# Row stores issued one at a time behind three points of a group, a pool of its own for the scores' two PSUM banks, and another order of slot 0's half blocks

## The chip, the cores and the metric

The kernel runs on one core of a Trainium2 chip. The metric is the device time of one execution in microseconds. The program schedules TensorE (PE), VectorE (DVE), ScalarE (ACT) and GpSimd (POOL) by hand: on each of these engines instructions run in the order in which the program writes them. SyncE (SP) only issues loads.

## The reference

Chunked softmax attention feeds a mixture of eight experts in which each row goes to one expert:

```python
# q, k, v: 8 x 8 heads x 576 x 64, chunks of 64
scores = scale * np.matmul(q_c, k_c.transpose(0, 1, 2, 4, 3))
attn = np.exp(scores - np.max(scores, axis=-1, keepdims=True))
attn = attn / (np.sum(attn, axis=-1, keepdims=True) + 1e-09)
x = np.matmul(attn, v_c)            # laid out as 4608 rows of 512
...
logits = x @ w_gate                 # 512 -> 8
expert_idx = np.argmax(logits, axis=1)
# gate_w: softmax of the logits at expert_idx
for e in range(E):
    xe = x[expert_idx == e]
    h = np.maximum(xe @ w1[e], 0.0) # 512 -> 1024
    out[expert_idx == e] = gate_w[...] * (h @ w2[e])
```

## The kernel before

**Attention.** The 4608 rows are 36 tiles of 128. A pass g of the loop `for g in range(NG)` (18 passes, here called groups) works on two tiles and holds three stages at once: the scores of g (64 small matmuls, L229, into the two banks of `pair["S"]`), then for group g-1 the transposes of its exponentials (`attn_t`, L272), the row sums (`soft_c`), and the weighted product (`attn_v`, 64 small matmuls, L281, into `pair["X"]`), and for group g-2 the transposes of its finished rows (`x_t`, L304) and the router's logits (`logits`, L316, copied to `lp`, L903). "The product of group 10" is the one that is issued in pass 10. The program also splits the first expert's weights into a high and a low part there: `cast(g)` lets ScalarE copy half a chunk (L81) and GpSimd subtract (L82), and issues the next load.

**Routing and row stores.** Tiles are routed in batches of 4, 8, 8, 4, 4, 4, 4. `route` is a generator whose steps (`"c"`, `"v"`, `"a"`, `"t"`) the program places by `advance` and `small_op`; after its last vector steps each tile of the batch stands in the list `waiting` with the row numbers `di`. `store(n, after)` takes n of them: GpSimd copies one column of `after` (L418), so that it waits for that tile, and then issues one indirect transfer a tile (L421) that scatters 128 rows of 528 floats to the DRAM tile `xd`, sorted by expert. A group has two such points, behind the row sums and behind the copy of the logits; each issues one store, or two when more than four tiles are waiting:

```python
store(2 if len(waiting) > 4 else 1, su[:, 0, :])
...
store(2 if len(waiting) > 4 else 1, st_l[gl][:, 0:1])
```

**The tail and slot 0.** The experts' rows are worked in slots of 256 rows. `early(0)` finds slot 0's rows when the first three batches are stored and gathers them (`gather(0)`, L541); `make_xt(0)` transposes them (L564) and splits them (`xhi` L566 on ScalarE, `xlo` L567 on VectorE, then `ids`, L555 and L556). `slot_0` is a generator: 16 steps in the order `BLOCKS`, a "1" step a block of the first gemm (12 matmuls, L584), a "2" step one of the second (6 matmuls, L660 to L662), each in two halves. `filler(n)` issues n halves between the steps of the last groups' attention and routing; `halves` counts those left. The last route, the stores of the last batch, the tables of slots (`tables`, L749 to L841), the gather of slot 1's extra rows (`gather_x(1)`) and the loads of the next expert's weights (`load_w`, L526) follow, and the remaining halves run beside them.

**Banks.** The eight PSUM banks are one pool `psa`: S and X of two banks, T, Q, L and K of one. Slot 0's first gemm alternates between a bank of S and T, its second gemm adds up in the two banks of X. Behind slot 0 the pool is closed and all eight banks are taken again under new names for the later slots, which run to the end: slot 1 begins with the transposes of its extra rows (`make_xt_x`, L573, bank T), their split (L575, L576) and the first gemm (`gemm1_x`, L591). `finish` (L666) scales a slot's result and scatters it to the output.

## Time and profile before

| | us |
|---|---|
| median of 3 runs | 650.45 (649.5 to 650.96) |
| the profiled execution | 648.89 |
| its span, first to last instruction | 647.1 |
| TensorE busy in the span | 591.4 |
| VectorE, ScalarE, GpSimd busy | 420.9, 286.5, 275.2 |
| mean granted clock of TensorE | 0.968 of full speed |

The attention groups take the first 135 us of the span, the tail with slot 0 the stretch to about 180 us, the later slots the rest. Times in the rows are microseconds from the start of the span; merged instructions of one line stand in one row with their count. "issue" as a releaser is time in which the engine waited for nothing that the profile shows, and a wait for several semaphores is put down to the one that came last by the profile.

### The profile page before, as it was taken

How to read it: one execution, taken by the hardware profiler on the slowest of the kernel's cores; microseconds unless marked ns; L12 is line 12 of the kernel's file. 1: busy time of each engine (PE TensorE's matmuls, PEld its weight loads, DVE VectorE, ACT ScalarE, POOL GpSimd, SP SyncE). 2: the span in 40 equal slices, each digit the busy share in tenths (PEclk: the TensorE clock that was granted, in tenths of full speed). 3: DMA queues.
4: the chain of work that ended last, by engine and by line, in shares of the span. 5: the costliest groups of instructions: out<-in, count | busy, mean ns of one | idle time of the engine just before them, and what ended most of it. 6: DMA issues, size and time to landing. Idle time of an engine off the chain costs nothing.

```text
span 647.1 us, 14596 instructions
## 1 busy us (share of the span) xinstructions
PE 591.4 (91%) x5775; PEld 518.6 (80%) x5775; DVE 420.9 (65%) x831; ACT 286.5 (44%) x523; POOL 275.2 (43%) x287
## 2 busy tenths in 40 slices
PE   7697898987979999999999999998999999999980
PEld 5575676766879989988798878997889999989970
DVE  6696868774556667765476566776547667767760
ACT  2465746552123445444354344553435545445530
POOL 2024345565514437434174143743407346437431
PEclk9899979789989999999999999999999999999995
DMA  8989789533465332146036211356602055111100
GB/s 324 375 282 364 256 294 297 194 118 122 159 226 169 135 116 81 55 147 213 6 111 222 82 38 44 106 209 229 206 2 91 18 181 183 58 49 35 34 5 30
DMA packets 31901, 94.87 MB, mean 147 GB/s; under 512 B 11488, under 2 KB 11488, under 8 KB 28192
## 3 DMA queue, kind: packets, MB, share of 16 engines
q0 software_dynamic: 20880, 60.74, 27.6%
q1 hardware_dynamic: 10896, 32.53, 14.3%
q8 instruction: 71, 1.16, 0.7%
q14 instruction: 54, 0.44, 0.2%
HBM read 122.65 MB, written 19.96 MB: 220 GB/s over the span
## 4 chain that ended last, share of the span: by engine, by line
PE 73%; issue 9%; DMA 8%; ACT 3%; DVE 2%; another core or an unknown queue 1%; POOL 1%; SPq 0%; POOLq 0%; DVEq 0%; ACTq 0%
PE psS L584 14%; PE psS L591 8%; DMA out_y<-y,oid 7%; PE psX L584 4%; PE psX L281 4%; PE psL L661 4%; PE psR L660 4%; PE psL L660 4%; PE psR L661 4%; PE psR L662 4%; PE psL L662 4%; PE psS L229 3%; PE psX L591 2%; PE psT L304 2%; PE psQ L304 1%
## 5 line engine op out<-in xcount | busy, mean ns | idle before, releaser
L75 DVE TENSOR_TENSOR wlo<-raw,whi 128x1024 fp32r<-128x1024 f32 x134 | 163.8, 1223 | 38.4 <-ACT whi L74 33.2
L526 POOL DMA_INDIRECT raw<-in_w,widx x71 | 73.7, 1038 | 195.9 <-DVE wlo L75 156.1
L74 ACT CAST whi<-raw 128x1024 fp32r<-128x1024 f32 x134 | 140.2, 1046 | 0.1
L604 ACT ACTIVATE hh<-psS 128x256 fp32r<-128x256 f32 x106 | 40.7, 384 | 171.7 <-PE psS L584 87.9
L584 PE MATMUL psS<-xlo,whi 128*128 128x256 f32 x328 | 92.9, 283 | 1.8 <-DVE xlo L567 1.8
L584 PE MATMUL psS<-xhi,whi 128*128 128x256 f32 x328 | 92.9, 283 | 0.5 <-DVE xlo L567 0.5
L584 PE MATMUL psS<-xhi,wlo 128*128 128x256 f32 x328 | 92.8, 283 | 0.0
L541 POOL DMA_INDIRECT xg<-xd,idx x58 | 81.5, 1405 | 22.9 <-issue 14.6
L609 DVE SCALAR_TENSOR_TENSOR hl<-psS,hh 128x256 fp32r<-128x256 f32 x106 | 44.8, 422 | 65.6 <-ACT hh L604 36.0
L667 POOL DMA_INDIRECT out_y<-y,oid x40 | 53.6, 1340 | 45.2 <-DVE y L666 39.7
L584 PEld LDWEIGHTS psS<-xlo,whi 128*128 128x128 f32 x328 | 62.6, 191 | 4.5 <-DVE xlo L567 2.0
L584 PEld LDWEIGHTS psS<-xhi,whi 128*128 128x128 f32 x328 | 62.6, 191 | 4.2 <-ACT xhi L566 0.7
L584 PEld LDWEIGHTS psS<-xhi,wlo 128*128 128x128 f32 x328 | 62.6, 191 | 0.0
L660 PE MATMUL psL<-whi,hh 128*128 128x512 f32 x136 | 55.0, 405 | 0.0
L661 PE MATMUL psL<-wlo,hh 128*128 128x512 f32 x136 | 53.8, 396 | 0.0
L660 PE MATMUL psR<-whi,hh 128*128 128x512 f32 x136 | 53.5, 393 | 0.0
L661 PE MATMUL psR<-wlo,hh 128*128 128x512 f32 x136 | 53.3, 392 | 0.0
L662 PE MATMUL psR<-whi,hl 128*128 128x512 f32 x136 | 53.1, 391 | 0.0
L662 PE MATMUL psL<-whi,hl 128*128 128x512 f32 x136 | 53.1, 391 | 0.0
L82 POOL TENSOR_TENSOR wlo<-raw,whi 128x512 fp32r<-128x512 f32 x16 | 20.4, 1276 | 61.4 <-ACT whi L81 61.4
L421 POOL DMA_INDIRECT xd<-xb,di x32 | 31.8, 994 | 15.1 <-issue 7.7
L281 PE MATMUL psX<-vb,at 64*64 64x64 f32 x1152 | 29.3, 235 | 8.1 <-issue 7.7
(237 smaller groups left out, 1218.1 us busy)
## 6 DMA issues: line engine op xcount, KB each, us to landing
vb<-in_v SPq DMA_DIRECT2D x18, 512.0 KB
kb<-in_k SPq DMA_DIRECT2D x17, 512.0 KB
qt<-in_q SPq DMA_DIRECT2D x17, 512.0 KB
raw<-in_w SPq DMA_DIRECT2D x16, 256.0 KB
raw<-in_w,widx POOLq DMA_INDIRECT x71
xg<-xd,idx POOLq DMA_INDIRECT x58
out_y<-y,oid POOLq DMA_INDIRECT x40
kb<-in_k SPq DMA_DIRECT2D x2, 256.0 KB
```

Source lines behind the costliest of these rows:

```text
L74: nc.scalar.copy(hi, src)
L75: nc.vector.tensor_tensor(lo, src, hi.bitcast(F32), ALU.subtract)
L281: nc.tensor.matmul(px[po, m, fo], at[pi, i, hp, po], vb[g % NB][pi, i, fi], start=True, stop=True, tile_position=at_)
L526: nc.gpsimd.indirect_dma_start(out=raw[c][:, :], out_offset=None, in_=w, in_offset=bass.IndirectOffsetOnAxis(ap=widx[:, u, c:c + 1], axis= ...
L541: nc.gpsimd.indirect_dma_start(out=t[:, :], out_offset=None, in_=xd[0:rows, :], in_offset=bass.IndirectOffsetOnAxis(ap=place(u, h), axis=0 ...
L584: nc.tensor.matmul(ph, a, b[:, kc, 0:BLK], start=kc + i == 0, stop=kc + i == 5)
L591: nc.tensor.matmul(ph, a[par][kc][:, f * 128:(f + 1) * 128], b[:, kc, 0:BLK + n], start=kc + i == 0, stop=kc + i == 5)
L609: nc.vector.scalar_tensor_tensor(hl, ph, 0.0, hh.bitcast(F32), ALU.max, ALU.subtract)
L660: nc.tensor.matmul(py, hh, wh, start=f == 0, stop=False)
L661: nc.tensor.matmul(py, hh, wl, start=False, stop=False)
L662: nc.tensor.matmul(py, hl, wh, start=False, stop=f == 7)
L667: nc.gpsimd.indirect_dma_start(out=outs[m], out_offset=bass.IndirectOffsetOnAxis(ap=oid[u % 3][0:n, m:m + 1], axis=0), in_=y, in_offset=No ...
```

## The change

Three things change together.

The stores: every point issues one store, however many tiles are waiting, and there is a third point in a group, behind the exponential of the group's own scores, used when more than two tiles are waiting. In the tail stores of two and of all waiting tiles become stores behind single tiles (the transposed exponentials, the row sums, the transposed rows, the logits), mostly one each; the last batch's are issued one for every two halves of slot 0, each behind a small copy on ScalarE (`tick`). `gather_x(1)` moves behind the first two weight loads. The weight halves are split one group earlier (`j = g - 1`), so that the last group splits none.

The banks: S has its own pool, closed behind the last maximum of the scores; its two banks then rotate for slot 0's first gemm and for the later slots. The other six banks stay as they are to the end: U and V (formerly the pair X) take the second gemm's sums in all slots, the later slots' third bank of the first gemm is L.

The half blocks: slot 0's first gemm uses the two S banks alone, and the halves between the steps of the tail are 1, 2, 1, 1, 1, 1, 2, 1, 1 in place of 1, 1, 2, 1, 1, 1, 1, so that 11 instead of 8 are issued before the loop that ends the tail. The last transposes of rows (`x_t`) stand behind one more of them.

```diff
--- before.py
+++ after.py
@@ -83,21 +83,24 @@
 
 
 
-    pa = ExitStack()
-    psa = pa.enter_context(tc.tile_pool(name="psa", bufs=1, space=PSUM))
-    pair = {x: psa.tile([P, 2, 512], F32, name=f"ps{x}") for x in "SX"}
+    psa = ctx.enter_context(tc.tile_pool(name="psa", bufs=1, space=PSUM))
+    pair = {"X": psa.tile([P, 2, 512], F32, name="psX")}
     one = {x: psa.tile([P, 512], F32, name=f"ps{x}") for x in "TQLK"}
-    slots = {"S": [pair["S"][:, 0, :], pair["S"][:, 1, :]], "X": [pair["X"][:, 0, :]],
-             "Y": [pair["X"][:, 1, :]], "TQ": [one["T"], one["Q"]], **{x: [one[x]] for x in "TQLK"}}
+    c2 = ExitStack()
+    pss = c2.enter_context(tc.tile_pool(name="pss", bufs=1, space=PSUM))
+    pair["S"] = pss.tile([P, 2, 512], F32, name="psS")
+
+    slots = {"U": [pair["X"][:, 0, :]], "V": [pair["X"][:, 1, :]], "X": [one["L"]],
+             "TQ": [one["T"], one["Q"]], **{x: [one[x]] for x in "TQLK"}}
     turns = {x: 0 for x in slots}
     psum = []
 
-    def bank(tag, shape, bufs=1):
+    def bank(tag, shape):
         n = 1
         for x in shape[1:]:
             n *= x
-        if psum:
-            t = psum[0].tile([P, 512], F32, name=f"ps{tag}", tag=tag, bufs=bufs)
+        if tag == "S":
+            t = psum[0].tile([P, 512], F32, name="psS", tag="S", bufs=2)
         else:
             t = slots[tag][turns[tag] % len(slots[tag])]
             turns[tag] += 1
@@ -130,7 +133,7 @@
     ones = const.tile([P, P], BF16, name="ones")
     nc.vector.memset(ones, 1.0)
 
-    pw = bank("X", [P, P])
+    pw = bank("U", [P, P])
     for _ in range(WARM):
         nc.tensor.matmul(pw, ones, ones, start=True, stop=True)
     iota_i = xg[0][0][:, 0:P].bitcast(I32)
@@ -190,6 +193,7 @@
     nc.gpsimd.memset(oh_b, 0.0)
 
     behind = kv.tile([P, 1], F32, name="behind")
+    moments = kv.tile([P, 16], F32, name="moments")
     cb = kv.tile([P, NBAT, E], F32, name="cb")
     ce = kv.tile([P, E, NBAT], F32, name="ce")
 
...
@@ -629,14 +633,14 @@
             f = BLOCKS[:i].count(step)
             flush()
             if step == "1":
-                ph = bank("ST"[f % 2], [P, BLK])
+                ph = bank("S", [P, BLK])
                 gemm1_pe(0, f, ph, range(2))
                 yield
                 gemm1_pe(0, f, ph, range(2, 4))
                 lo_.append((ph, relu_hi(ph)))
             else:
                 if py is None:
-                    py = [bank(x, [P, D]) for x in "XY"]
+                    py = [bank(x, [P, D]) for x in "UV"]
                 gemm2(0, f, h0[f], 0, py)
                 yield
                 gemm2(0, f, h0[f], 1, py)
@@ -917,7 +921,7 @@
 
     def cast(g):
 
-        j = g - 2
+        j = g - 1
         if 0 <= j < 16:
             split_half(j // 2, j % 2, j // 4 % 2)
         j = g + 1
@@ -937,13 +941,19 @@
         if ga >= 0:
             at = attn_t(st_e[ga])
             su = soft_c(st_e.pop(ga))
-            store(2 if len(waiting) > 4 else 1, su[:, 0, :])
+            store(1, su[:, 0, :])
         if gl >= 0:
             st_x[gl] = x_t(gl, xb[gl * G // RB % XB])
         st_e[g] = soft_a(ps)
         if g + 1 < NG:
             soft_b(st_e[g])
+            if len(waiting) > 2:
+                store(1, st_e[g][:, 0, 0, 0:1])
             cast(g)
+        else:
+
+            c2.close()
+            psum.append(ctx.enter_context(tc.tile_pool(name="psum", bufs=1, space=PSUM)))
         advance("t")
         pauses()
         if g + 1 < NG:
@@ -953,10 +963,9 @@
         logits(gl)
         if g + 1 == NG:
             soft_b(st_e[g])
-            cast(g)
         if ga >= 0:
             if gl >= 0:
-                store(2 if len(waiting) > 4 else 1, st_l[gl][:, 0:1])
+                store(1, st_l[gl][:, 0:1])
             ri = soft_d(su)
             x_out(ga, px, ri, xb[ga * G // RB % XB])
         small_op(2)
@@ -970,50 +979,63 @@
     g = NG - 1
     sel_(g - 2)
     advance("c")
-    make_xt(0, banks="SX")
+    make_xt(0, banks="SS")
     small_op(5)
     ex = st_e.pop(g)
     at = attn_t(ex)
-    store(2)
+    store(1, at[:, 0, 0, 0:1])
     filler(1)
     su = soft_c(ex)
+    store(1, su[:, 0, :])
     advance("a")
     st_x[g - 1] = x_t(g - 1, xb[(g - 1) * G // RB % XB])
+    store(1, st_x[g - 1][:, 0, 0:1])
     pauses()
     small_op(7)
     advance("a")
     px = attn_v(g, at)
-    filler(1)
+    filler(2)
     ri = soft_d(su)
     x_out(g, px, ri, xb[g * G // RB % XB])
+    logits(g - 1)
+    store(1, st_l[g - 1][:, 0:1])
+    filler(1)
     advance("t")
-    logits(g - 1)
     small_op(5)
     advance("a")
-    store(NMAX)
-    filler(2)
-    flush()
+    filler(1)
     st_x[g] = x_t(g, xb[g * G // RB % XB])
+    store(2, st_x[g][:, 0, 0:1])
     sel_(g - 1)
+    filler(1)
     side_op(4)
     logits(g)
-    side_op(4)
-    pauses()
+    store(2, st_l[g][:, 0:1])
+    assert stored.issuperset(range(TE[1]))
     filler(1)
     sel_(g)
     advance("c")
-    filler(1)
+    side_op(4)
+    pauses()
+    filler(2)
     pauses()
     small_op(7)
     advance("a")
     filler(1)
-    side_op(5)
     advance("t")
     filler(1)
     small_op(5)
     advance("a")
-    store(NMAX)
-    assert len(stored) == NTILE
+    side_op(5)
+    ticks = [0]
+
+    def tick():
+
+        t = moments[:, ticks[0]:ticks[0] + 1]
+        nc.scalar.copy(t, pid[:, 0:1])
+        ticks[0] += 1
+        return t
+
     while active:
         for x in "cat":
             advance(x)
@@ -1022,7 +1044,10 @@
         side_op(3)
         if halves[0] > 5:
             filler(1)
-    gather_x(1)
+        if halves[0] % 2:
+            store(1, tick())
+    store(NMAX)
+    assert len(stored) == NTILE
     load_w(2, 0)
     load_w(2, 1)
 
@@ -1035,20 +1060,17 @@
     yp = ctx.enter_context(tc.tile_pool(name="yp", bufs=1))
     hx = ctx.enter_context(tc.tile_pool(name="hx", bufs=HB))
     hq = ctx.enter_context(tc.tile_pool(name="hq", bufs=1))
+    filler(2)
+    gather_x(1)
+    filler(2)
     for c in range(2, 4):
         load_w(2, c)
     filler(halves[0] - 4)
-    make_xt(1, banks="QT")
+    make_xt(1, banks="QK")
     filler(5)
-    pa.close()
-    psum.append(ctx.enter_context(tc.tile_pool(name="psum", bufs=1, space=PSUM)))
-
-    for tag, n in (("S", 2), ("L", 1), ("R", 1), ("Q", 1), ("K", 1), ("T", 1), ("X", 1)):
-        bank(tag, [P, 512], n)
-
     def slot(u, kd, nxt):
         par = wset(u)
-        py = [bank("LR"[m], [P, D]) for m in range(2)]
+        py = [bank("UV"[m], [P, D]) for m in range(2)]
         if u > 1:
             gather(u + 2)
```

## Rows read from the trace of the kernel before

**Rows 1.** The page's second part: TensorE's busy time and its granted clock in tenths, in 40 slices of the span.

```profile
PE   7697898987979999999999999998999999999980
...
PEclk9899979789989999999999999999999999999995
```

**Rows 2.** The table of windows, all engines: the stretch in us from the span's start, its length, then for PE, PEld, DVE, ACT and POOL the busy us and the number of instructions, the granted clock of TensorE, the busy share of the transfer engines, and GB/s.

```profile
78.50:92.00 13.50, 11.45 (x225) 9.10 (x228) 6.50 (x9) 6.22 (x12) 6.68 (x9) 0.75 0.91 318
...
92.00:109.00 17.00, 15.74 (x415) 12.70 (x407) 16.02 (x32) 11.08 (x27) 8.14 (x13) 1.00 0.86 272
...
109.00:122.00 13.00, 11.23 (x233) 9.36 (x235) 9.07 (x26) 6.58 (x13) 6.47 (x10) 0.74 0.66 227
...
187.00:280.00 93.00, 93.00 (x565) 84.67 (x565) 63.20 (x126) 42.24 (x72) 42.84 (x34) 1.00 0.32 103
```

**Rows 3.** The timeline of TensorE through the attention groups: start, duration of the merged instructions, line, operands, count, and in brackets the idle time before and what ended it.

```profile
27.96 0.49 PE L272 MATMUL psT<-ident,ex 128*128 128x128 f32 x3 [2.88 <-issue]
...
72.27 1.16 PE L281 MATMUL psX<-vb,at 64*64 64x64 f32 x64
...
73.36 0.64 PE L316 MATMUL psL<-xT,wg_sb 128*32 128x256 f32 x8
...
78.51 0.93 PE L281 MATMUL psX<-vb,at 64*64 64x64 f32 x41
...
83.10 0.64 PE L316 MATMUL psL<-xT,wg_sb 128*32 128x256 f32 x8
...
83.67 1.98 PE L229 MATMUL psS<-kb,qt 64*64 64x64 f32 x64
...
92.33 1.20 PE L229 MATMUL psS<-kb,qt 64*64 64x64 f32 x64
...
98.00 0.50 PE L281 MATMUL psX<-vb,at 64*64 64x64 f32 x15 [0.38 <-issue]
...
99.00 1.16 PE L229 MATMUL psS<-kb,qt 64*64 64x64 f32 x64
...
109.05 0.80 PE L281 MATMUL psX<-vb,at 64*64 64x64 f32 x38
...
113.36 0.64 PE L316 MATMUL psL<-xT,wg_sb 128*32 128x256 f32 x8
...
126.41 0.80 PE L281 MATMUL psX<-vb,at 64*64 64x64 f32 x37
...
128.77 0.64 PE L316 MATMUL psL<-xT,wg_sb 128*32 128x256 f32 x8
```

**Rows 4.** The timeline of GpSimd: three of the stores of attention rows (the first and the fourth of group 9 and 10, and one of group 12).

```profile
77.09 1.00 POOL L421 DMA_INDIRECT xd<-xb,di  x1
...
81.02 0.99 POOL L421 DMA_INDIRECT xd<-xb,di  x1 [0.30 <-issue]
...
96.70 0.99 POOL L421 DMA_INDIRECT xd<-xb,di  x1 [0.55 <-issue]
```

**Rows 5.** The timelines of GpSimd, VectorE and TensorE around the first gather and the transposes of slot 0's rows.

```profile
126.75 0.99 POOL L421 DMA_INDIRECT xd<-xb,di  x1 [0.16 <-issue]
...
130.70 1.04 POOL L541 DMA_INDIRECT xg<-xd,idx  x1 [0.73 <-PE psS L229]
...
138.91 1.30 POOL L82 TENSOR_TENSOR wlo<-raw,whi 128x512 fp32r<-128x512 f32 x1
...
138.60 1.64 DVE L556 SCALAR_TENSOR_TENSOR oid<-msk,xg 128x1 int32<-128x1 f32 x1
...
136.82 0.60 PE L564 MATMUL psX<-ident,xg 128*128 128x128 f32 x4
...
140.90 0.39 PE L584 MATMUL psS<-xlo,whi 128*128 128x256 f32 x1 [1.77 <-DVE xlo L567]
```

**Rows 6.** First the chain of work that ended last, where slot 0's half blocks run without a wait (start, us, what); then the timelines of TensorE and ScalarE at the last route.

```profile
163.92 1.44 PE psS L584 x12
...
166.75 1.43 PE psT L584 x12
...
153.08 0.51 PE L894 MATMUL psL<-sel_g,lp 128*128 128x8 f32 x4
...
158.07 0.18 PE L376 MATMUL psK<-oh_b,tri 128*128 128x40 bf16 x1 [2.96 <-DVE oh_b L357]
...
156.71 0.18 ACT L340 COPY lg<-psL 128x32 f32<-128x32 f32 x1 [3.81 <-remote]
```

**Rows 7.** The timelines of GpSimd (the last stores, gather_x) and TensorE (slot 0's last matmul and slot 1's first), then one row of the table of windows.

```profile
163.73 1.05 POOL L421 DMA_INDIRECT xd<-xb,di  x1 [2.57 <-DVE tot L766]
...
167.67 0.97 POOL L421 DMA_INDIRECT xd<-xb,di  x1 [0.30 <-issue]
...
171.26 1.05 POOL L541 DMA_INDIRECT xg<-xd,idx  x1 [2.62 <-DVE kind L841]
...
178.46 0.39 PE L662 MATMUL psX<-whi,hl 128*128 128x512 f32 x1
...
181.41 0.63 PE L573 MATMUL psT<-ident,xg 128*128 128x128 f32 x4 [2.56 <-DVE y L666]
...
182.75 1.65 PE L591 MATMUL psS<-xhi,whi 128*128 128x384 f32 x4 [0.72 <-ACT xhi L575]
...
178.00:180.00 2.00, 0.85 (x4) 0.38 (x2) 0.98 (x4) 0.59 (x1) 0.00 (x0) 1.00 0.98 401
```

More of the change, by code (lines that the diff above doesn't have):

```diff
@@ L561, in make_xt @@
         for h in range(2) if part is None else (part,):
-            pg = bank(banks[h], [P, 4, 128], 2 if banks == "SS" else 1)
+            pg = bank(banks[h], [P, 4, 128])
             for kc in range(4):
@@ L586, in gemm1_x @@
     def gemm1_x(par, f, n, hh=None, hl=None):
-        ph = bank("X", [P, BLK + n]) if f % 3 == 2 else bank("S", [P, BLK + n], 2)
+        ph = bank("X", [P, BLK + n]) if f % 3 == 2 else bank("S", [P, BLK + n])
         for i, (a, b) in enumerate(((w_hi, xhi), (w_lo, xhi), (w_hi, xlo))):
@@ L612, in gemm1 @@
     def gemm1(par, f, hh=None, hl=None):
-        ph = bank("X", [P, BLK]) if f % 3 == 2 else bank("S", [P, BLK], 2)
+        ph = bank("X", [P, BLK]) if f % 3 == 2 else bank("S", [P, BLK])
         gemm1_pe(par, f, ph)
```

## The prediction

> **What bounds the kernel now.** I read the page first: TensorE is busy in nearly every slice, but not in the first third, where the granted clock also dips [rows 1]. The table of windows says how to split that third: between the disturbed stretches the clock stands at 1.00, in 78.5 to 92 and 109 to 122 us it averages 0.75 and 0.74, and from 187 us on TensorE is busy all the time at full clock [rows 2]. So a microsecond saved before 187 us is a microsecond at the end, and nothing can be saved behind it. Then I took TensorE's timeline through the attention groups. A group's weighted product (64 small matmuls, L281) takes 1.09 us from its start to the next matmul where nothing disturbs it; in group 10 it breaks into pieces, "issue" before each, and needs 78.51 to 83.10, which is 4.59 us; in group 14 it needs 109.05 to 113.36, 4.31 us; in group 16 2.36 us; in group 12 one gap of 0.38 us [rows 3]. GpSimd's timeline beside it shows what these have in common: four stores without a pause around the product of group 10, one store beside that of group 12 [rows 4]; the product at 72.27, with no store near, is whole. Behind the two long breaks the granted clock is at the lower of its two levels, 1.2 GHz: the scores at 83.67 take 1.98 us where those at 99.00 take 1.16, and from the scores at 83.67 to the next at 92.33 it is 8.66 us, from there to 99.00, with one gap taken off, 6.29 us. Last, the tail: TensorE waits 1.77 us for xlo, 2.96 us for route's one-hot, 2.56 and 0.72 us at the start of slot 1 [rows 5 to 7].
>
> **The change, part by part.** The profiled execution took 648.89 us (span 647.1); the median of the runs is 650.45, so 1.56 is added at the end.
>
> *Stores, one at a time.* Their number, bytes and issue time stay (36 of about 1 us each on GpSimd). Followed by hand, the eight stores of a large batch leave at eight points of groups 9 to 12 (13 to 16), one each, and the last leaves at the same point of the same group as before; no point has two. What is there to gain is 3.50 us (group 10), 3.22 (group 14), 1.27 (group 16), 0.38 (group 12), and the lower clock, 2.4 in group 11 and, estimated from the equal clock of the two windows [rows 2] and a little lower because routing's matmuls share that group, 2.0 in group 15: 12.8 us in all. What takes its place: the store behind the row sums still falls on the weighted product in groups 10, 11, 12, 14, 15 and 16. One alone costs 0.38, which I put on group 12; in the other five the store of the logits' point before it is adjacent, and I take two gaps, 0.8: 5 x 0.8 + 0.4 = 4.4. The new point, behind the exponential, lies just ahead of the next group's scores, which are 64 matmuls of the same kind: five such stores at 0.38 are 1.9. That leaves 6.3, a gain of 6.5 us. Bounds: all 17 stores at the price of group 10 (3.50 / 4 = 0.88) and the clock down twice (4.4) make 19.4, a loss of 6.6; six single gaps and nothing at the scores make 2.3, a gain of 10.5. I take the middle because the nearest row, group 12, has single stores in just this place. The extra one-column copies (at most 0.2 us each) and the split that now stands behind them delay only GpSimd: who waits for the split's result is slot 0, tens of microseconds later.
>
> *Weight halves split one group earlier.* The same 16 splits; the loads run groups ahead, except the first, which has nine loads of 0.5 MB ahead of it on SP (4.7 MB, some 12 us at the 400 GB/s of [rows 7]) and lands about when group 1 wants it: 0 to 1 us of ScalarE's time, which then still waits for transposes. I take 0. What goes is the split in group 17: there the oid step of VectorE took 1.64 us until GpSimd's split at 138.91 was over, and TensorE waited 1.77 for the xlo behind it [rows 5].
>
> *Slot 0's rows.* gather(0) waits until every store ahead of it has landed: the store at 126.75 ended at 127.74, the gather began at 130.70, 2.96 later [rows 5]. In the new order group 16 has one more store, behind its exponential, ahead of the gather. I place its end near 129.5, so the gather begins near 132.4, 1.7 later; its second half, 1.35 behind, ends its issue near 134.7 and would land some 3 us later, near 137.7, where TensorE wants it at 136.8 [rows 5]. Against that stand 0.5 on ScalarE and 1.5 on VectorE from the missing split. Net about 1 us of the 1.77 is saved, and, as an estimate, 1 us of lower clock behind it; but the last weighted product now runs at full clock beside a queue of stores, and I charge 1.0. Net 1 us, bounds -2 and +4.
>
> *Half blocks laid anew.* Ten halves instead of seven stand ahead of the last route's matmuls. A half costs 0.71 us (two steps from 163.92 to 166.75 [rows 6]), so they cover 2.1 of the 2.96 wait; two buffers for the half blocks instead of a bank shared with x_t remove a wait of x_t for hl. ScalarE's copy of the logits came 3.1 us late although TensorE had finished ("remote", [rows 6]); it may come late again. 2.1 of cover, the idle 2.96 and some slow clock behind it are 6 to 7; I take 5 us, bounds 2 and 8. With the 1 us above, slot 0's last matmul would end at 178.9 - 6 = 172.9 [rows 7].
>
> *Banks that stay.* L573 waited for y only because all banks changed hands at once; bank T is now free, so 2.56 us would go. But gather_x is now behind two weight loads on GpSimd's queue. Followed through [rows 7]: the last batch's stores had to wait for gather(1) and began at 163.73. gather(1) needs the stores behind the last logits, which I place 2.4 us earlier (half of the 5, as the logits stand in the middle of the stretch), so the four stores run 161.3 to 166.3; load_w issues at 166.6 and 167.9; the stores have landed 2.6 later (171.26 less 168.64), so gather_x issues at 169. If transfers go in order of issue, 2.1 MB at some 390 to 400 GB/s [rows 7] from about 168.2 keep it until 173.6, and it lands at 174.5; if not, it lands 3 us after its issue, at 172.2. The Trainium skill ("DMA: Bandwidth & Descriptors", section "Queues, rings and completion order") says that an engine consumes descriptors in ring order, which speaks against this part; by it the sum goes by 174.5, otherwise slot 1 starts 2.3 us sooner. No row above shows two such transfers in one queue. I take 174.5, the later: then slot 1's first gemm starts at 174.5 + 1.3 = 175.8 instead of 182.75, a gain of 7 us for the whole tail. Bounds: 1.4 (gather_x no sooner than now and behind the loads) and 9.7. The 5 + 1 us before it are not added: they only bring TensorE to this wait. Paced stores (an extra ScalarE copy of about 0.2 us each) cost nothing, since GpSimd is still waiting for gather(1) when the fourth copy is due.
>
> **Sum.** 648.9 - 6.5 - 7.0 = 635.4, on the median's footing 637.0.
>
> **Rivals.** (1) *The breaks are not the stores'.* TensorE also stood 2.88 us in "issue" at 25 us, with no store issued yet [rows 3]. If it is its instruction stream that is late when the transfer engines are full, spacing stores leaves the breaks where they are: only the tail's 7.0 remains, 643.5. The Trainium skill ("Runtime: NRT & Kernel Launch", section "Instruction fetch mechanics") has the stream refilled in blocks by transfers of its own, mostly hidden; by it neither the 2.88 nor the breaks would be refills, and the trace's 2.88 leaves that open. For it: the transfer engines are at 0.91 in 78.5 to 92. Against: at 0.86, in 92 to 109 [rows 2], products lose at most 0.38. (2) *Tail gives nothing*: gather_x late and the clock down again, 1.4 instead of 7.0: 642.6. (3) *Slower: every store breaks a burst.* Three points a group put stores on the products and on the scores; at 0.88 for each of 17 stores (15.0) and the clock down in five groups at 2.2 (11) the stretch costs 26 instead of 12.8, which the tail's 7.0 doesn't cover: 656.7. It decides from 19.8 us, 1.17 per store with the clock. For it: the stores at 0.88 in group 10; against: no clock fall behind a single gap. (4) *The change doesn't do what it says*: GpSimd is so late that the stores go back to back as before, and gather_x waits: about 650.
>
> **How the numbers follow.** Forecast 0.56 (its own range 630 to 643.5, from the bounds that are likely together), rival 1 0.14, rival 2 0.11, rival 3 0.12, rival 4 0.07. A measurement of this kernel tells about 0.2% (1.3 us) from no change. Faster: 0.56 + 0.14 + 0.11 + a little of rival 4 = 0.82; same 0.06; slower 0.12. Range 629 to 650: it leaves out rival 3 and what is better than both upper bounds by half.
>
> **What would show it.** In the changed profile: no four stores in a row on GpSimd before the tail; the products of groups 10 and 14 under 2 us and a clock of 0.9 or more in those stretches; gaps of some 0.4 us in the scores of groups 11, 12, 15 to 17; no split in group 17 and an oid step of 0.2 us; L573 waiting for gather_x, not for y, and slot 1's first gemm about 13 us sooner than 182.75. I am wrong in the cause if the products stay broken with a single store beside them, and in the tail if L573 starts right behind slot 0's last matmul.

## The result and the profile after

The changed kernel takes 652.79 us, median of 20 runs (650.48 to 660.72), beside 650.07 for the kernel before in the same comparison (20 runs, 646.72 to 652.06): the ratio is 1.0055, with an interval of 1.0033 to 1.0077. It is half a per cent slower, where I had forecast 2% faster, and lies outside my range. The profiled execution of the changed kernel took 655.06 us with a span of 652.9, so 5.8 more than the span of 647.1 before. A second pair of profiles on another chip (runs 9 and 10 below) differs by 5.7 (646.1 and 651.8).

Two lines per kernel are enough to see where the 5.8 lie: a pass's router sums (`sel_`), which are the same four matmuls in both. First the kernel before, TensorE's timeline, at pass 10 and behind the loop:

```profile
75.54 0.61 PE L894 MATMUL psL<-sel_g,lp 128*128 128x8 f32 x4 [0.45 <-ACT lp L903]
...
135.88 0.61 PE L894 MATMUL psL<-sel_g,lp 128*128 128x8 f32 x4 [0.55 <-ACT lp L903]
```

Then the changed kernel, the same view and the same two places, and from there slot 0's last matmul and slot 1's first ones:

```profile
76.81 0.61 PE L898 MATMUL psL<-sel_g,lp 128*128 128x8 f32 x4 [0.45 <-ACT lp L907]
...
135.96 0.61 PE L898 MATMUL psL<-sel_g,lp 128*128 128x8 f32 x4 [0.83 <-ACT lp L907]
...
175.51 0.39 PE L666 MATMUL psX<-whi,hl 128*128 128x512 f32 x1
184.70 1.11 PE L577 MATMUL psT<-ident,xg 128*128 128x128 f32 x4 [8.80 <-DMA xg<-xd,idx]
186.49 1.65 PE L595 MATMUL psS<-xhi,whi 128*128 128x384 f32 x4 [0.68 <-ACT xhi L579]
```

| stretch | before, us | after, us | difference | forecast |
|---|---|---|---|---|
| start to pass 10's router sums | 75.54 | 76.81 | +1.27 | 0 |
| groups 10 to 17 | 60.34 | 59.15 | -1.19 | -6.5 |
| to slot 0's last matmul | 42.97 | 39.94 | -3.03 | -6.0 |
| from there to slot 1's first gemm | 3.90 | 10.59 | +6.69 | -1.0 |
| from there to the end | 464.35 | 466.41 | +2.06 | 0 |

(The forecast's -7.0 for the tail stands in two rows here, 172.9 for slot 0's last matmul and 175.8 for slot 1's first gemm.) So the half blocks brought half of what I gave them, and the wait for slot 1's rows ate it twice over: TensorE stood 8.80 us for xg, where it had stood 2.56 for y [rows 7]. GpSimd's timeline shows the queue in which that gather stands:

```profile
162.83 1.07 POOL L545 DMA_INDIRECT xg<-xd,idx  x1 [2.56 <-DVE kb L755]
...
172.85 0.98 POOL L425 DMA_INDIRECT xd<-xb,di  x1 [0.16 <-issue]
174.14 1.06 POOL L530 DMA_INDIRECT raw<-in_w,widx  x1 [0.30 <-issue]
175.50 1.01 POOL L530 DMA_INDIRECT raw<-in_w,widx  x1 [0.30 <-issue]
176.81 1.00 POOL L545 DMA_INDIRECT xg<-xd,idx  x1 [0.30 <-issue]
```

Two loads of 1 MB go first, and the rows land 7.84 us behind the gather's issue (184.65). In the kernel before this gather was issued at 171.26, ahead of the loads [rows 7]. And the last store is 5.2 us later than before (172.85, before 167.67), because gather(1) ahead of it is 4.5 later (162.83, before 158.34). Most of the reason stands in TensorE's timeline of the last weighted product; GpSimd's stores beside it follow:

```profile
140.85 0.73 PE L285 MATMUL psX<-vb,at 64*64 64x64 f32 x33
141.92 0.35 PE L285 MATMUL psX<-vb,at 64*64 64x64 f32 x4 [0.34 <-issue]
142.71 0.35 PE L285 MATMUL psX<-vb,at 64*64 64x64 f32 x4 [0.44 <-issue]
143.47 0.34 PE L285 MATMUL psX<-vb,at 64*64 64x64 f32 x4 [0.42 <-issue]
144.19 0.36 PE L285 MATMUL psX<-vb,at 64*64 64x64 f32 x6 [0.38 <-issue]
144.92 0.49 PE L285 MATMUL psX<-vb,at 64*64 64x64 f32 x4 [0.36 <-issue]
145.65 0.51 PE L285 MATMUL psX<-vb,at 64*64 64x64 f32 x6 [0.23 <-issue]
146.38 0.48 PE L285 MATMUL psX<-vb,at 64*64 64x64 f32 x3 [0.22 <-issue]
...
140.51 0.99 POOL L425 DMA_INDIRECT xd<-xb,di  x1 [0.16 <-issue]
142.10 0.98 POOL L425 DMA_INDIRECT xd<-xb,di  x1 [0.16 <-POOL behind L422]
143.44 0.99 POOL L425 DMA_INDIRECT xd<-xb,di  x1 [0.16 <-issue]
144.79 0.99 POOL L425 DMA_INDIRECT xd<-xb,di  x1 [0.16 <-issue]
```

After the first 33 matmuls the product goes on in handfuls, with about 0.4 us of "issue" between them, until 146.8: 6.0 us; in the kernel before this product went through whole in 2.31 at the lower clock (143.27, granted clock 0.57), although two stores (142.17 and 143.47) stood beside it. In the changed kernel the clock falls behind it: it is 0.50 from 146.8 on, and the next twelve half-block matmuls take 2.86 us, where they take 1.43 at full clock [rows 6].

In the attention groups the windows read as forecast; the columns are those of [rows 2]:

```profile
78.50:92.00 13.50, 11.00 (x281) 8.32 (x282) 9.92 (x12) 7.80 (x16) 8.95 (x13) 1.00 0.92 309
...
109.00:122.00 13.00, 10.52 (x287) 8.17 (x279) 12.27 (x27) 6.94 (x17) 7.09 (x11) 1.00 0.67 236
```

The clock is 1.00 in both, where it was 0.75 and 0.74 [rows 2]. But the products are not whole. TensorE's timeline, the product and the scores of group 10, then the product of group 16:

```profile
79.78 1.21 PE L285 MATMUL psX<-vb,at 64*64 64x64 f32 x48
81.37 0.52 PE L285 MATMUL psX<-vb,at 64*64 64x64 f32 x16 [0.38 <-issue]
...
82.38 1.37 PE L233 MATMUL psS<-kb,qt 64*64 64x64 f32 x50
84.12 0.48 PE L233 MATMUL psS<-kb,qt 64*64 64x64 f32 x14 [0.37 <-issue]
...
123.43 0.91 PE L285 MATMUL psX<-vb,at 64*64 64x64 f32 x43
124.55 0.47 PE L285 MATMUL psX<-vb,at 64*64 64x64 f32 x13 [0.22 <-issue]
125.35 0.30 PE L285 MATMUL psX<-vb,at 64*64 64x64 f32 x3 [0.32 <-issue]
126.08 0.39 PE L285 MATMUL psX<-vb,at 64*64 64x64 f32 x5 [0.42 <-issue]
```

### The profile page after: what moved, and what is told of

Read it like the earlier page. It is cut to its first block, busy times and chain, and to the rows that moved or that the text cites. A ratio compares the mean times of both kernels' runs of the same rounds, so it can differ in the third digit from the quotient of the medians.

```text
span 652.9 us, 14592 instructions
## 1 busy us (share of the span) xinstructions
PE 593.6 (91%) x5775; PEld 518.3 (79%) x5775; DVE 422.7 (65%) x831; ACT 287.2 (44%) x529; POOL 275.6 (42%) x302
## 3 DMA queue, kind: packets, MB, share of 16 engines
q8 instruction: 71, 1.16, 0.7%
## 4 chain that ended last, share of the span: by engine, by line
PE 69%; DMA 11%; issue 9%; DVE 5%; ACT 2%; POOL 1%; POOLq 0%; SPq 0%; DVEq 0%; ACTq 0%
PE psS L588 15%; PE psS L595 8%; PE psX L664 8%; PE psX L665 8%; PE psX L666 8%; DMA out_y<-y,oid 7%; PE psL L588 4%; PE psX L285 4%; PE psL L595 2%; PE psS L233 2%; DMA raw<-in_w 2%; PE psT L308 1%; DMA xg<-xd,idx 1%; PE psL L898 1%; PE psK L665 1%
## 5 line engine op out<-in xcount | busy, mean ns | idle before, releaser
L664 PE MATMUL psX<-whi,hh 128*128 128x512 f32 x288 | 115.2, 400 | 0.0
L665 PE MATMUL psX<-wlo,hh 128*128 128x512 f32 x288 | 113.4, 394 | 0.0
L666 PE MATMUL psX<-whi,hl 128*128 128x512 f32 x288 | 112.5, 391 | 0.0
L588 PE MATMUL psS<-xhi,whi 128*128 128x256 f32 x344 | 98.3, 286 | 0.0
L588 PE MATMUL psS<-xlo,whi 128*128 128x256 f32 x344 | 98.0, 285 | 0.3 <-DVE xlo L571 0.3
L588 PE MATMUL psS<-xhi,wlo 128*128 128x256 f32 x344 | 97.9, 285 | 0.0
L588 PEld LDWEIGHTS psS<-xlo,whi 128*128 128x128 f32 x344 | 66.4, 193 | 3.2 <-DVE xlo L571 0.5
L666 PEld LDWEIGHTS psX<-whi,hl 128*128 128x128 f32 x288 | 54.1, 188 | 12.2
L664 PEld LDWEIGHTS psX<-whi,hh 128*128 128x128 f32 x288 | 54.5, 189 | 8.1 <-issue 0.4
L665 PEld LDWEIGHTS psX<-wlo,hh 128*128 128x128 f32 x288 | 54.5, 189 | 6.9
```

What stands on the lines that cost most here:

```text
L588: nc.tensor.matmul(ph, a, b[:, kc, 0:BLK], start=kc + i == 0, stop=kc + i == 5)
L664: nc.tensor.matmul(py, hh, wh, start=f == 0, stop=False)
L665: nc.tensor.matmul(py, hh, wl, start=False, stop=False)
L666: nc.tensor.matmul(py, hl, wh, start=False, stop=f == 7)
```

## The experiments

Sixteen runs on four chips. Each group of four runs shares a chip and its runs of the kernel before, so only ratios are compared across groups. Ratios are to the kernel before, with 95% intervals.

| run | what it is | ratio |
|---|---|---|
| 1 | changed, gather_x first | 0.9971 (0.9943 to 0.9999) |
| 2 | changed, quiet last product | 1.0016 (0.9986 to 1.0045) |
| 3 | changed, old splits | 0.9979 (0.9953 to 1.0005) |
| 4 | before, attention's stores alone | 0.9944 (0.9913 to 0.9974) |
| 5, another chip | runs 1 and 2 together | 1.0113 (1.0079 to 1.0147) |
| 6 | runs 1, 2 and 3 together | 1.0081 (1.0056 to 1.0107) |
| 7 | run 6, old attention stores | 1.0043 (1.0017 to 1.0070) |
| 10, a third chip | the changed kernel | 1.0086 (1.0054 to 1.0117) |
| 11 | run 6, last rows stored early | 0.9942 (0.9918 to 0.9966) |
| 12 | run 4 again | 0.9970 (0.9939 to 1.0002) |
| 14, a fourth chip | run 11 again | 0.9930 (0.9905 to 0.9955) |
| 15 | run 14, old attention stores | 0.9983 (0.9959 to 1.0006) |
| 16 | run 1 again | 0.9978 (0.9950 to 1.0007) |

Runs 8, 9 and 13 were executed once each (648.35, 647.98 and 648.27 us).

### Run 1: the gather ahead of the loads

```diff
     store(NMAX)
+    gather_x(1)
     load_w(2, 0)
...
-    gather_x(1)
```

> The changed kernel, with the gather of slot 1's rows put straight behind the last row store, ahead of the loads of slot 2's weights; nothing else moves. My theory: in the changed kernel slot 0 ends at 175.9 us and TensorE then waits 8.8 us for these rows, because their gather stands behind two loads of 1 MB on GpSimd's queue. The gather would start at 172.85 + 3.6 = 176.4 us (the distance from the last store to this gather in the kernel before: 167.67 to 171.26) and land some 4 us later, as the second gather did there (159.69 issued, next store at 163.73). Slot 1's transposes then start near 180.5 instead of 184.70: 4 us less, and up to 2 more if the clock falls less in the shorter wait, 647 to 649 us. Rival (the rows land late for another reason, such as the stores before the gather or the DMA engines being full anyway): the wait for them stays within 1 us of 8.8, and the time stays at 652 to 653 us.

TensorE's timeline of this kernel:

```profile
179.20 0.66 PE L577 MATMUL psT<-ident,xg 128*128 128x128 f32 x4 [3.98 <-DMA xg<-xd,idx]
```

The wait fell from 8.80 to 3.98 us, slot 1's transposes came 5.5 us sooner, and the median is 648.63. The gather was issued at 175.67 and landed 3.5 us later, instead of 7.84 later behind the two loads. My theory holds; the rival is out. Run 16 gave 179.39 with a wait of 4.00.

### Run 2: no store beside the last product

```diff
     at = attn_t(ex)
-    store(1, at[:, 0, 0, 0:1])
     su = soft_c(ex)
-    store(1, su[:, 0, :])
...
-    store(1, st_x[g - 1][:, 0, 0:1])
     px = attn_v(g, at)
...
     logits(g - 1)
-    store(1, st_l[g - 1][:, 0:1])
+    store(4, st_l[g - 1][:, 0:1])
```

> The changed kernel, with the three row stores between the last weights' transposes and the last weighted product taken from there and issued with the next one, four in a row behind the last but one group's logits. My theory: the last product (140.9 to 146.8 us, in ten pieces) is broken by the stores that GpSimd issues beside it; with the queue empty from 141.5 on it ends near 144, the clock does not fall behind it, and slot 1 starts 2 to 4 us sooner: 649 to 651 us, with slot 1 still waiting 8 us or so for its rows. Rival (the product is broken by something else, such as the fetch of TensorE's instructions): it stays at 5 to 6 us, the four stores come 1 to 2 us later, and the time is 652 to 655 us.

TensorE's timeline of this kernel:

```profile
140.35 1.56 PE L285 MATMUL psX<-vb,at 64*64 64x64 f32 x64
...
180.70 1.12 PE L577 MATMUL psT<-ident,xg 128*128 128x128 f32 x4 [6.85 <-DMA xg<-xd,idx]
```

The product is whole: 1.56 us instead of 6.0. Slot 1's transposes start 4.0 us sooner, and the loads still hold its rows for 6.85 us. The median of 652.25 lies outside the 649 to 651 us expected; by the two ratios it is 0.39% (2.5 us) below the changed kernel, but their intervals overlap. So the profile shows the cause, and the time shows its worth only roughly.

### Run 3: the splits as before

```diff
-        j = g - 1
+        j = g - 2
...
             soft_b(st_e[g])
+            cast(g)
```

> The changed kernel, with the splits of the first weights laid one group later again, as in the kernel before (with their last one in the last group). My theory: the first split's wait for its load held TensorE for 0.8 us at 20.74 and no more; groups 1 to 9 run 0.8 to 2.0 us later than in the kernel before mostly because one transposed q landed 1.3 us later and a lower clock followed a stall of fetching. So this edit alone gives 0 to 1 us at group 9, and costs 0.5 to 1.5 us at the front of slot 0, where the last split stands in the way of the ids again: 652 to 654 us. Rival (the early splits cost the groups 1.5 to 2 us through the loads): groups 2 to 9 come 1.3 to 2 us sooner than in the changed kernel and the time is 651 us or less.

The ratio is 0.76% below that of the changed kernel, which I had not expected: the time is on the rival's side, but the profile does not show the rival's reason. Its profile (653.54 us, 4 above this kernel's median) does not give the gain to the first groups: pass 10's router sums come at 77.08. In the profiles of the kernels with early splits on chips where stores break products they come at 76.61 on average (six profiles: 76.05 to 76.91), with the old splits at 75.88 (eight: 74.41 to 77.08): 0.7 us, inside the "0 to 1" of the prediction. What did differ is the last product, which lies in two pieces here (143.05 and 144.40): the old last split, 1.33 us at 141.50 on GpSimd, delays the stores, so that only two (143.12 and 144.72) fall on it. That is run 2's gain by another road. That it is all of this run's gain is argued, not shown.

### Run 4: the attention's stores alone

The kernel before, with the three lines of the change's loop that issue stores.

> The kernel before, with only the attention's stores changed: issued singly, and a third point behind the group's exponentials where more than two wait; banks, splits, tail and slot 0 as before. My forecast of the attention part by itself was 6.5 us less (643.5 us). By the trace of the changed kernel groups 10 to 17 took only 1.2 us less than before (59.15 for 60.34 us from the router sums of the seventh group to the last): the pieces of groups 10 and 14 became whole, but groups 16 and 17 lost 3 us to stores that are now spread into them. My theory now: 1 to 3 us less than before, 647 to 649 us. Rival (the change's other parts, such as the banks, slowed the groups): 643 to 645 us.

645.32 us, 3.6 less than before by the ratio, slightly more than I expected and half of the forecast. But its profile (span 641.6) shows no more of that in the groups than the changed kernel does: from pass 10 to the tail 59.86 us. From there to slot 1's first gemm it is 4.4 us shorter (42.46, before 46.87), although nothing in the tail was changed. ScalarE's timeline tells why in this execution: it stalls there for 3.4 us as it does in the kernel before (3.81, [rows 6]), but one instruction later, behind the copy of the logits on which the last route waits, not ahead of it:

```profile
153.73 0.18 ACT L340 COPY lg<-psL 128x32 f32<-128x32 f32 x1 [0.91 <-PE psL L894]
157.28 0.39 ACT L604 ACTIVATE hh<-psS 128x256 fp32r<-128x256 f32 x1 [3.37 <-issue]
```

So a single profile's total mixes an edit's effect with where such a stall falls. Run 12, the same kernel on a third chip, gave 0.9970, and in its profile the stretch that is 42.46 here takes 46.84 (136.03 to 182.87), as in the kernel before.

### Runs 5 to 8: a chip on which stores break next to nothing

Run 5 has the edits of runs 1 and 2, run 6 those of runs 1 to 3. Run 7 is run 6 with the old attention stores:

```diff
-            store(1, su[:, 0, :])
+            store(2 if len(waiting) > 4 else 1, su[:, 0, :])
...
-            if len(waiting) > 2:
-                store(1, st_e[g][:, 0, 0, 0:1])
...
-                store(1, st_l[gl][:, 0:1])
+                store(2 if len(waiting) > 4 else 1, st_l[gl][:, 0:1])
```

> The changed kernel with both of the first two edits: slot 1's gather straight behind the last row store, and no row store beside the last weighted product. My theory: the two causes follow one another (the product ends 4 us sooner, so the last stores, slot 0's end and the gather all come sooner), so the gains add: 5.5 us of the one by its median and 2.5 to 4 us of the other; TensorE waits 3 to 4 us for the rows behind slot 0's last matmul at about 172, and the time is 643 to 646 us. Rival (the gains are one and the same, because the gather is then late for what stands ahead of it): 647 to 649 us.

> The changed kernel with all three edits: gather first, no store beside the last product, and the splits of the first weights one group later, as in the kernel before. The splits alone took 4.9 us off by the medians, which I had not expected, and whose place its profile doesn't show: in it groups 1 to 9 run no sooner, and the last product lies in two pieces where the changed kernel has ten, because the last split keeps GpSimd from its stores just then. Theory: that is where its gain was, and it is taken here already by the quiet product: 643 to 647 us, within 2 us of the kernel with two edits. Rival (the splits' loads hold up the first groups or the weights in a way that one profile doesn't show): 638 to 641 us.

> The kernel of all three edits with the attention's stores as in the kernel before (up to two behind a point where more than four wait, and no third point): banks, tail and half blocks of the change alone. My theory, from the kernel before with the attention's part alone (3.6 us less, 1.7 to 5.7): it is 2 to 5 us slower than the kernel of three edits, 646 to 650 us. My forecast for that part would make it 6.5 us slower. Rival (that kernel gained by where its stalls fell in the tail, not in the attention): within 1 us of the kernel of three edits.

All three kernels are slower than the kernel before, which takes 641.09 us on this chip (median of 21 runs), 9 less than on the others; so the expected times, which were made for chips at 650, say little here. Run 5 lies in its rival's range, run 6 in its theory's, and run 7 is faster than run 6, where both its theory and my forecast had it slower. GpSimd's and TensorE's timelines of run 7, group 10, with four stores in a row, as in the kernel before:

```profile
77.70 1.01 POOL L425 DMA_INDIRECT xd<-xb,di  x1
79.01 0.98 POOL L425 DMA_INDIRECT xd<-xb,di  x1 [0.30 <-issue]
80.34 0.98 POOL L425 DMA_INDIRECT xd<-xb,di  x1 [0.16 <-issue]
81.63 0.98 POOL L425 DMA_INDIRECT xd<-xb,di  x1 [0.30 <-issue]
...
79.10 1.16 PE L285 MATMUL psX<-vb,at 64*64 64x64 f32 x64
```

The same stores at the same distance leave the product whole, where in the kernel before it took 4.59 us [rows 3, 4]. Groups 10 and 14 take 5.99 and 6.69 us, beside 10.03 and 9.30 in the kernel before: 6.7 less, which is what the forecast laid on these two breaks (3.50 and 3.22). Groups 10 to 17 together take 55.74 us in run 7, beside 60.34, 61.32 and 59.66 in three profiles with the same store points on chips with breaks. That is only 4.7 less on average, but it is not the price of the breaks, because group 11 is longer in run 7: 11.52 us, in the kernel before 7.89. TensorE stands still there once, between two transposes, and behind that the granted clock is 0.50 from 86 to 92 us:

```profile
86.33 0.48 PE L276 MATMUL psQ<-ident,ex 128*128 128x128 f32 x1 [2.78 <-issue]
```

Runs 5 and 6 have a stall at the same matmul (2.35 and 2.63 us); what causes it, no run shows. The other seven groups are 8.2 us shorter than in the kernel before. And on that chip the single stores gain nothing: run 6 is 0.38% slower than run 7. Run 6 stayed within 2 us of run 5, as the theory had it. Why the new tail is 0.4 to 1.1% slower than the old one on that chip stays open: no profile of the kernel before was taken there. One part is seen: from the last store of the last but one batch to gather(1) it is 4.5 to 4.8 us there (3.73 in the kernel before and in run 1), so the chain of stores and gathers is longer, and TensorE waits 7.3 to 7.6 us for slot 1's rows even with the gather first.

Run 8 put four plain copies of 256 KB, on SyncE's queue, into the place of the stores beside the last product:

```diff
     at = attn_t(ex)
+    nc.sync.dma_start(scr[0], at[:, 0, :, :].rearrange("p a b -> p (a b)"))
...
+    for i in range(1, 4):
+        nc.sync.dma_start(scr[i], st_x[g - 1][:, i - 1:i + 1, :].rearrange('p a b -> p (a b)'))
```

> The changed kernel without stores beside the last weighted product, as in the second experiment, and with four plain copies of 256 KB each, of the transposed weights and of the transposed rows, issued on SyncE's queue to a scratch in DRAM in their place: as many bytes to DRAM beside the product as the row stores moved, and no descriptors made by GpSimd. This adds work and moves the stores. Theory: the pieces of 0.73 us come from GpSimd's indirect issues, not from the bytes; the product stays whole, 2.2 to 3 us. Rival (the traffic to DRAM breaks it): it is in three or more pieces and takes 4 us or more.

On this chip, where the row stores do not break the product either, it decides nothing. Run 13 is the same kernel on a chip with breaks.

### Runs 9 to 12: both kernels and the mended one on a third chip

> The kernel before, once more, for its profile on the chip that the other three of this call share. In the four runs before these (another chip than the first four) no weighted product and no scores were broken, beside however many stores: 64 matmuls in 1.16 us, where the first chip's runs took 1.6 to 5.9. Theory: whether GpSimd's stores break TensorE's small matmuls differs from chip to chip; on a chip like the second, this kernel's groups 10 and 14 take 6 to 7 us each, and the time is near 641 us, on one like the first they take 9 to 10, and it is near 650. Rival: the breaks come from the stores' place alone, and groups 10 and 14 of this kernel take 9 to 10 us on any chip.

> The changed kernel, once more. Theory: where stores break nothing, its attention part has nothing to gain, and only its late gather is left, 6 to 10 us slower than the kernel before (about 648 to 651 us beside 641); where they break the products, 1 to 5 us slower, as before (652 beside 650). Rival (the change's cost is the broken product): on a chip without breaks it is no slower than the kernel before.

> The changed kernel of the three edits (gather first, no store beside the last product, splits a group later), and with the rows of the last but one batch stored as soon as their places are known, ahead of the last rows' transposes, as in the kernel before, not held behind these transposes and the last logits. My theory: the chain of stores, gather, stores and gather on GpSimd's queue sets the start of slot 1; in the sixth run the last store of that batch was issued 20.9 us behind the router sums at 134.85 (155.73), in the kernel before 18.7 behind them (154.61 behind 135.88); held by nothing it comes 3 us sooner, and with it the gather, the rows and slot 1: TensorE's wait for the rows falls from 7.6 to 4 or 5 us, and the time to 3 us under that of the three edits: 1.003 to 1.005 of the kernel before on a chip without breaks, 0.985 to 0.99 on one with. Rival (the chain waits for the routing's arithmetic, not for the points): the wait stays within 1 us of 7.6 and the time the same.

> The kernel before with the attention's stores alone changed, once more. Theory: its gain (3.6 us) was the stores' breaks of the products; on a chip without breaks it is within 1 us of the kernel before, 0.9985 to 1.002; on one with, 0.991 to 0.997 again. Rival (it gained by where stalls of fetching fell in the tail): 0.993 to 0.997 on any chip.

Here stores break products again: group 10 takes 10.3 us in run 9 (75.75 to 86.07). The two profiles repeat the table above, and run 10 is 0.86% slower than the kernel before, slightly more than the 1 to 5 us expected: groups 10 to 17 take 61.32 and 59.20, the wait for slot 1's rows is 7.93 us, and behind slot 1's first gemm the changed kernel takes 466.8 us beside 463.0.

Run 11 adds one line to run 6:

```diff
     advance("a")
+    store(NMAX)
     filler(1)
     st_x[g] = x_t(g, xb[g * G // RB % XB])
```

It beats both kernels, 0.58% below the kernel before (expected on such a chip: 1 to 1.5%), but not by its reason. The last store of the batch still comes 20.6 us behind the router sums, as in run 6 (20.9): it stands behind seven others that GpSimd issues one after the other from 146.83 on, so I take their number to set it, and not the points. My theory for that line falls. The gain then is that of the three edits, on a chip where the product can be broken; that is argued, since run 6 itself was not run on such a chip. Its wait for rows was 2.43 us.

### Runs 13 to 16: what was still open, on a fourth chip

> The kernel of the eighth run once more (no row stores beside the last weighted product, four plain copies of 256 KB on SyncE's queue to a scratch in DRAM in their place), which on its chip said nothing, since there nothing was broken. On a chip where stores break products: theory, the pieces come from GpSimd's indirect issues, and the product beside the plain copies is whole or in two pieces, 1.2 to 2.5 us; rival, the traffic to DRAM breaks it, four pieces or more and 3.5 us or more (six to ten pieces beside the row stores of the changed kernel). On a chip that breaks nothing: no verdict.

> The kernel of the eleventh run once more (gather first, no store beside the last product, splits a group later, last rows stored early): 0.9942 of the kernel before, 0.9918 to 0.9966, on a chip with breaks. Theory: 0.991 to 0.997 again on such a chip; on one without breaks 1.000 to 1.005. Rival (the eleventh run's ratio was luck): 0.998 or more on a chip with breaks.

> The same kernel with the attention's stores as in the kernel before (two behind a point, no third point). Theory: on a chip with breaks the single stores gain 1 to 2 us between the seventh group's router sums and the last of the loop (59.2 to 59.8 us with them, 60.3 and 61.3 without), so this kernel is 1 to 3 us slower than the one beside it; on a chip without breaks the same or up to 3 us faster. Rival (my forecast of the attention part, 6.5 us): 5 to 8 us slower.

> The changed kernel with slot 1's gather first, once more, to set it beside the kernel of all edits on one chip. In its first run it was 0.9971 of the kernel before (0.9943 to 0.9999). Theory: 0.995 to 1.000 on a chip with breaks, 2 to 4 us slower than the kernel of all edits, whose last product is whole and whose rows come earlier; 1.009 or more on a chip without. Rival (the gather's place is all that mattered): within 1 us of the kernel of all edits.

The timelines of TensorE and SyncE in run 13:

```profile
140.94 1.54 PE L286 MATMUL psX<-vb,at 64*64 64x64 f32 x64
...
138.78 0.33 SPq L987 DMA_DIRECT2D scr<-at  x1
142.31 2.03 SPq L993 DMA_DIRECT2D scr<-xT  x3
```

The product stayed whole, 0.4 us longer than an undisturbed one, on a chip where the product of group 17, beside GpSimd's gather, is in three pieces in the same profile. But it was not the test that I meant: three of the four copies were issued when the product was all but over. What it does show comes from elsewhere. The row store issued at 140.24 and the one before it were still moving their bytes: in the table of DMA queues GpSimd's queue (q0) carries 0.42 MB from 140.9 to 142.5, 264 GB/s, beside a product that is whole. The kernel before shows the reverse, in the same table for the broken product of group 10 (78.5 to 83.1 us; queue, packets, MB, share of the engines):

```profile
q1 hardware_dynamic: 356, 1.16, 84.6%
q0 software_dynamic: 22, 0.09, 4.9%
```

While three stores were issued (78.40, 79.74 and 81.02) their queue moved next to nothing, and SyncE's loads (q1) moved less in a microsecond than beside the whole product at 72.27 (0.32 MB in 1.09 us, with no store near). So neither the loads' bytes nor the stores' own break the product; what is left is GpSimd's issuing of the stores. How that reaches TensorE, no run shows.

Run 14 repeats run 11's gain (644.44 beside 649.82 us). GpSimd's and TensorE's timelines:

```profile
172.43 1.06 POOL L545 DMA_INDIRECT xg<-xd,idx  x1 [2.58 <-DVE oid L560]
...
175.95 1.12 PE L577 MATMUL psT<-ident,xg 128*128 128x128 f32 x4 [2.92 <-DMA xg<-xd,idx]
```

Run 15, without the single stores, is 0.53% slower, 3.2 us by the medians: that is the attention part's worth in the time, beside 3.6 (run 4) and 1.9 (run 12). The positions in the profiles show less: 60.4 on average with the old points (three profiles), 59.6 with the single ones (eleven). Where the other 2 us come from I could not place. Run 16, the gather alone mended, is 0.48% slower than run 14 (2.4 us by the medians). Against the changed kernel's 1.0055 and 1.0086 the gather's place is about two thirds of what run 14 gains (0.84 of 1.25% with the result and run 1, 1.08 of 1.56% with runs 10 and 16; ratios from several chips), the quiet product and the splits the rest.

## Why the prediction was wrong, step by step

- **Stores, one at a time: right in place, the price of a single store wrong.** By the time they were worth 1.9 to 3.6 us (runs 4, 12, 15; run 12's interval takes in no change), not 6.5. The terms for groups 10 and 14 held: 10.03 to 7.72 and 9.30 to 6.61 us, 5.0 together, forecast 5.1 (3.50 and 3.22 less 0.8 each). What failed is the 6.3 us for what takes the breaks' place, and in it "one alone costs 0.38". That is only the gap ahead of the second piece of group 12's product. TensorE's timeline of the kernel before has the first piece and what follows the product:

```profile
96.37 1.25 PE L281 MATMUL psX<-vb,at 64*64 64x64 f32 x49
...
98.43 0.64 PE L316 MATMUL psL<-xT,wg_sb 128*32 128x256 f32 x8
```

The first 49 matmuls alone take longer than all 64 of an undisturbed product, at a granted clock of 1.00 in both. From its start to the next matmul this product takes 2.06 us instead of 1.09, so a single store costs 0.97. In the changed kernel the products with one gap (groups 10, 11, 12, 14 and 15) take 1.99 to 2.04 us, those of 16 and 17, which have three gaps and two, 2.96 and 2.74. All products together lose 8.2 us where I had 4.4, and the scores of groups 10, 11 and 16 lose 3.0 where I had 1.9. These 4.9 us are most of the 5.3 by which groups 10 to 17 missed the forecast. With 0.97 at each of its eleven places the forecast's own sum would have given a gain of 2.7, an estimate from these rows. The clock did come back in groups 11 and 15 (1.00, before 0.68 and 0.64), but the new gaps took what it gave (7.89 to 7.99, 8.05 to 8.41), in group 15 together with a stall of 1.31 us among the transposes ("issue", 114.86). Groups 16 and 17 lost 3.0 us (6.93 to 8.06, 5.45 to 7.37): the batch's last stores and the gather fall on them.
- **Rival 1 (the breaks are not the stores').** False where products break: there the breaks go with GpSimd's issues (run 2, and the queues' bytes shown with run 13). On one chip of four the same issues break next to nothing.
- **Splits earlier.** Taken as 0; by the positions 0.7 us, within the bound. But the split in group 17 that I counted as a hindrance also kept stores off the last product (run 3).
- **Slot 0's rows.** The step itself came as forecast: no split in group 17, the wait for xlo 0.28 us instead of 1.77. The charge of 1.0 for the last product beside a queue of stores is the term that failed: 6.0 us instead of 2.31, and the lower clock behind it, 1.43 us in the next half block alone. Run 2 shows the worth, 4.0 us at slot 1's start. I had charged 1.0 for the disturbance without a row for it.
- **Half blocks.** The 2.96 wait for the one-hot is gone, as forecast. Slot 0's last matmul came 3.0 us sooner, not 6. The broken product is about half of the difference: in run 2, where it is whole, that matmul comes 4.6 sooner, and where the other 1.4 stayed is open.
- **Banks that stay.** L573's successor waits for the rows and not for y, as forecast, and the rows land in order of issue: 7.84 us behind the loads, 3.5 without (run 1). I had chosen that branch, and the rule that I quoted for it agrees: by the Trainium skill ("DMA: Bandwidth & Descriptors", section "Queues, rings and completion order") an engine consumes descriptors in ring order. The page says it of the queues of SyncE and ScalarE; that GpSimd's queue behaves alike, these two landings show. What failed is the time from which I counted. I placed gather(1) 2.4 us earlier, near 155.9; it was issued at 162.83, so the stores ended at 173.8 instead of 166.3 and the gather was issued at 176.8 instead of 169. The product ahead of the last logits is 3.8 of these 6.9 us: behind the router sums at the loop's end gather(1) comes 26.9 us in the changed kernel, 23.1 in run 2, where the product is whole, and 22.5 in the kernel before. So even without the break it would not have come sooner than before: in run 2 eight stores go out in a row from 145.53 to 154.80, and gather(1) follows the last as far behind as in the kernel before. What that queue costs by itself no run isolates. The step "slot 1's first gemm at 175.8" fell by 10.7 us: 7.8 for the later issue, 2.3 for the landing (7.84 us, forecast 5.5), the rest for a start at the lower clock.
- **Rival 2** had the mechanism (gather late, clock down) with a gain of 1.4 left. In fact slot 1 started 3.7 later, and from its first gemm to the end another 2.1 went, part of it to the clock: the first gemm runs at the lower level until about 192, and the windows around 460 us stand at 0.91 and 0.92 (1.00 in the kernel before). **Rival 3** had the sign and, with 0.88 for a store, nearly the price, but not the place: the clock did not fall in the loop, which lost nothing on the whole, and the loss was in the one product that is followed by the tail's chain and in the place of the gather.

## What to carry to other kernels

When a change moves work onto a queue that a later transfer shares, follow that transfer from the earliest link of its chain, not from where the chain stood before: here one product stretched by 3.7 us moved the three links behind it, and a gather put behind two loads added 4.3 more. What a disturbance costs is read from the whole stretch beside an undisturbed one, here 0.97 us, and not from the gap that the trace prints, 0.38. A run in which the disturbance is absent helps only as far as nothing else has come in, as the stall in group 11 of run 7 did. And medians on one chip do not carry over to another, so kernels that are compared share a chip.

## What I had not expected of the hardware

On three of the four chips of these runs (and on that of the result) GpSimd's indirect issues broke TensorE's 64x64 matmuls into handfuls with gaps of 0.2 to 0.5 us; on one chip the same kernels' products went through in 1.16 us beside four stores in a row (with a gap of 0.35 us once, in group 13 of run 5), and the kernel before took 641 instead of 650 us. A product at the lower clock, the kernel before's last, stayed whole beside two stores. TensorE's longest stall ("issue") in the first 200 us is 1.5 to 3.7 us in every profile; ScalarE has one of 3.2 to 3.8 us near the last route in four (the kernel before, runs 4, 11 and 15). Whether such a stall comes there changes between profiles of one kernel: 3.37 us in run 4, none over 1.3 us in run 12.
